# Gated linear attention and a cosine-gated feed-forward: two transposes per chunk moved from the tensor engine to the DMA queues

## The chip, the cores and the metric

The kernel runs on one core of a Trainium2 chip. The metric is the device time of one execution in microseconds (us); the time before is the median of three runs, 201.37 us (200.56 to 201.77). One execution was profiled; the engines are PE (matrix multiply; PEld are its weight loads), DVE (VectorE), ACT (ScalarE), POOL (GpSimd) and SP, which only issues DMAs and waits.

## What is computed

For each of 4 batches and 8 heads, a recurrence over 768 steps with a 48 x 48 state gives y; the heads' outputs, joined to 3072 rows of 384, pass through a feed-forward with a cosine gate. Inputs and output are float32.

```
for t in range(S):
    state = alpha[:, :, t, :, None] * state + np.einsum('bhd,bhe->bhde', k[:, :, t], v[:, :, t])
    y[:, :, t] = np.einsum('bhd,bhde->bhe', q[:, :, t], state)
...
h = x @ w_in          # 384 -> 2048
g = h * np.cos(h)
return (g @ w_out)    # 2048 -> 384
```

## The kernel before

The steps are cut into 24 chunks of 128 (six for each batch). Every chunk goes through the same units of work, and each unit is named by letters and the chunk's number j (or the pair's number g = j // 2):

- Loads on the SP queue (L98, L102): `a`, `k`, `q`, `v`, 192 KB each, 96 in all; alpha has four buffers of two chunks, the others six of one. `z` and `Z` (L109, L122) load the two weight matrices in four quarters of 768 KB each; `r`, `s`, `R` cast them to bf16.
- Decay: `i`/`l` take the logarithm of alpha on ACT (L142), `c`/`C` sum it along the chunk by a triangular matmul (L155, L159), `d`/`E` take exp of plus and minus the sum on ACT (L173, L175). `E_` (L198) keeps the last row's decay for the state.
- `K` and `Q` (L183, L189, POOL) scale k and q and write bf16 into one of three buffers, `khb` and `qhb`; `b` (L193) casts v.
- `T` (L211) transposes khb and qhb on PE, eight 128 x 128 blocks into one PSUM bank, and `t` (L217, DVE) copies the 128 x 1024 result to SBUF.
- `A` (L228) makes the scores, `m` (L237, DVE) masks them; `S` (L250) makes the chunk's contribution to the state, `u` (L262 DVE, L264 POOL) adds and decays the state; `Y` (L279, L282) makes the chunk's output from the state and the scores; `y` (L289, DVE) casts it to bf16.
- `D` (L298) transposes y on PE, three blocks, and `B` (L303, DVE) copies the result to SBUF as x.
- Feed-forward: `F` and `G` (L315) are the two halves of x @ w_in, 24 matmuls each; `f_`/`g_` (L323) the sine on ACT, `p`/`Q_` (L329) the gate on DVE; `V` and `W` (L337) the two halves of the second product, 8 matmuls each; `e` (L342, ACT) copies the result out of PSUM, and the store (L343) is issued on the SP queue.
- `w` (L353) are idle matmuls on zeros that keep PE busy at the start.

`T`, `S`, `Y` and `D` share one PSUM bank (tag `g`), the second product has one (`o`), and scores, sums and first products take turns in three buffers of two banks (`big`).

The order is written out by hand in a string, ORDER: the units are recorded in that order, and each engine, and each engine's DMA queue, takes its own ones strictly in that order. A unit starts when its engine has done the earlier ones and the semaphores it waits for have come. Eight semaphores are dealt out in turn to the DMAs that SP and ACT issue, in the order of the program, so a DMA is issued only when the one eight places before it has landed.

```
    for u in ORDER.split():
        nm = u.rstrip("0123456789")
        units[nm](int(u[len(nm):]))
```

Of the kernel before, what the change touches and what calls it, by code (L numbers as in the profile page):

```python
# [10 lines left out]
BF = mybir.dt.bfloat16  # L11
AF = mybir.ActivationFunctionType
ALU = mybir.AluOpType
# [3 lines left out]
def kernel(  # L17
# [10 lines left out]
    nc = tc.nc  # L28
    B, H, S, D = q.shape
    DM, DF = moe_w_in.shape  # L30
    C = 128
    NC = S // C
    NCH = B * NC
    NP = H // 2
    NF = DF // C
    HF = NF // 2
    HD = H * D
    CW = HD + NP
    ACOL = [(h % 2) * NP + h // 2 for h in range(H)]
    PF = 6  # L40
# [5 lines left out]
    work = ctx.enter_context(tc.tile_pool(name="work", bufs=2))  # L46
# [19 lines left out]
    qhb = consts.tile([C, 3, H, 64], BF, tag="qhb")  # L66
    khb = consts.tile([C, 3, H, 64], BF, tag="khb")
# [6 lines left out]
    ub = consts.tile([C, 3, NP, 96], BF, tag="ub")  # L74
# [3 lines left out]
    m2 = consts.tile([C, 2], FP, tag="m2")  # L78
# [5 lines left out]
    w1 = consts.tile([C, 3, DF], BF, tag="w1")  # L84
    w2f = consts.tile([C, NF, DM], FP, tag="w2f")
    w2 = consts.tile([C, NF, DM], BF, tag="w2")
# [61 lines left out]
    def cums(j0, n):  # L148
# [5 lines left out]
        for i in range(lo, lo + n):  # L154
            nc.tensor.matmul(  # L155
                cum_ps[g][:, i, 0:HD], triu_bf, lnab[:, g % 2, i, :, 0:D], start=True, stop=True
            )
            for p in range(NP):
                nc.tensor.matmul(  # L159
                    cum_ps[g][:, i, HD + p : HD + p + 1],  # L160
                    lnab[:, g % 2, i, 2 * p : 2 * p + 2].rearrange("s h d -> s (h d)"),
# [39 lines left out]
        )  # L201
        Em_t[j] = Em

    qkT_ps, qkT_t = {}, {}

    def transposes(j):
        t = ps.tile([C, 2 * NP * C], BF, tag="g")
        qkT_ps[j] = t
        for i, src in enumerate((khb, qhb)):
            for p in range(NP):  # L210
                nc.tensor.transpose(  # L211
                    t[:, (i * NP + p) * C : (i * NP + p + 1) * C],
                    src[:, j % 3, 2 * p : 2 * p + 2].rearrange("s h d -> s (h d)"), ident_bf)

    def ev_transposes(j):
        t = work.tile([C, 2 * NP * C], BF, tag="qkT", bufs=3)
        nc.vector.tensor_copy(out=t, in_=qkT_ps.pop(j))  # L217
        qkT_t[j] = t

    A_ps, A_t = {}, {}  # L220

    def scores(j):
        t = ps.tile([C, H * C], FP, tag="big", bufs=3)
        A_ps[j] = t
        for h in range(H):
            base = 64 * (h % 2)
            p = h // 2
            nc.tensor.matmul(  # L228
                t[:, ACOL[h] * C : (ACOL[h] + 1) * C],
                qkT_t[j][base : base + D, p * C : (p + 1) * C],  # L230
                qkT_t[j][base : base + D, (NP + p) * C : (NP + p + 1) * C],
                start=True, stop=True,
            )

# [7 lines left out]
        A_t[j] = t  # L242

    U_ps = {}

    def state(j):
        t = ps.tile([C, 512], FP, tag="g")
# [8 lines left out]
    def ev_state(j):  # L256

        t = U_ps.pop(j)[:, 0 : NP * 96].rearrange("r (p e) -> r p e", p=NP)
        sc = t
        if j % NC != 0:  # L260
            sc = work.tile([C, NP, 96], FP, tag="sc")
            nc.vector.tensor_tensor(out=sc, in0=t, in1=ub[:, (j - 1) % 3, :, 0:96], op=ALU.add)  # L262
        eng = nc.vector if j % NC == 0 else nc.gpsimd
        eng.tensor_tensor(  # L264
            out=ub[:, j % 3, :, 0:96].rearrange("r p (a e) -> r p a e", a=2),
            in0=sc.rearrange("r p (a e) -> r p a e", a=2),
            in1=Em_t.pop(j).unsqueeze(3).to_broadcast([C, NP, 2, D]), op=ALU.mult,
        )

    y_ps, x_t = {}, {}  # L270

    def outputs(j):
        t = ps.tile([C, 512], FP, tag="g")
        y_ps[j] = t
        first = j % NC == 0
        qT = qkT_t[j]
        for p in range(NP):
            if not first:
                nc.tensor.matmul(t[:, p * 96 : (p + 1) * 96], qT[:, (NP + p) * C : (NP + p + 1) * C],  # L279
                                 ub[:, (j - 1) % 3, p], start=True, stop=False, skip_group_check=True)  # L280
            for h in (2 * p, 2 * p + 1):
                nc.tensor.matmul(t[:, h * D : (h + 1) * D], A_t[j][:, ACOL[h] * C : (ACOL[h] + 1) * C],  # L282
                                 vpb[:, j % 3, h], start=first, stop=True, skip_group_check=True)

    y_t, xT_ps = {}, {}

    def ev_outputs(j):
        t = work.tile([C, HD], BF, tag="y_sb")
        nc.vector.tensor_copy(out=t, in_=y_ps.pop(j)[:, 0:HD])  # L289
        y_t[j] = t  # L290
        qkT_t.pop(j)
        A_t.pop(j)

    def x_transposes(j):
        t = ps.tile([C, 3, C], BF, tag="g")
        y = y_t.pop(j)
        for kt in range(3):
            nc.tensor.transpose(t[:, kt], y[:, kt * C : (kt + 1) * C], ident_bf)  # L298
        xT_ps[j] = t
# [40 lines left out]
    def ev_ff2(j):  # L340
        o_sb = moe.tile([C, DM], FP, tag="o_sb", bufs=3)
        nc.scalar.activation(out=o_sb, in_=o_ps.pop(j)[:, 0:DM], func=AF.Copy)  # L342
        nc.sync.dma_start(out=out[j * C : (j + 1) * C, :], in_=o_sb)  # L343

    w_t = []

    def warmup(n):
# [14 lines left out]
        "i": lambda j: ln(j, 1), "c": lambda j: cums(j, 1), "d": lambda j: exps(j, 1),  # L362
        "l": lambda g: ln(2 * g, 2), "C": lambda g: cums(2 * g, 2), "E": lambda g: exps(2 * g, 2),
        "K": khat, "Q": qhat, "b": vcast, "E_": emask,
        "T": transposes, "t": ev_transposes, "S": state, "u": ev_state,
        "A": scores, "m": mask_scores, "Y": outputs, "y": ev_outputs, "D": x_transposes, "B": ev_x,

# [3 lines left out]
    }  # L371

    ORDER = (
        "a0 i0 q0 q1 a1 c0 v0 d0 Q0 i1 w11 c1 d1 k0 k1 K0 w9 T0 t0 K1 a2 a3 w4 A0 v1 Q1 w1 T1 t1 b0 m0 w9 Y0 "
        "E_0 y0 A1 w2 S0 l1 C1 E1 b1 u0 q2 w1 S1 a4 a5 k2 Q2 v2 k3 E_1 E_2 l2 w9 C2 m1 E2 u1 K2 a6 a7 Y1 y1 "
        "w3 D0 b2 B0 w2 D1 B1 K3 q3 w2 S2 l3 u2 w3 T2 t2 w4 A2 Q3 T3 C3 t3 q4 Q4 m2 k4 K4 E3 w4 T4 t4 z0 s0 "
        "A3 w2 A4 z1 r1 v3 Y2 r0 s1 w1 F0 m3 m4 E_3 E_4 E_5 z2 z3 y2 F1 b3 r2 D2 B2 f_0 p0 f_1 s2 w2 S3 F2 s3 "
        "q5 u3 r3 Q5 p1 Y3 G0 G1 v4 b4 f_2 k5 y3 K5 D3 p2 B3 G2 g_0 Q_0 g_1 g_2 Z1 Z0 Y4 F3 Q_1 y4 R0 Z2 D4 "
        "G3 B4 R1 V0 f_3 T5 Q_2 F4 p3 Z3 g_3 R3 k6 K6 q6 t5 Q6 v5 v6 b5 A5 a8 S4 f_4 R2 E_6 W0 m5 a9 a10 u4 "
        "a11 b6 T6 t6 Q_3 e0 V1 W1 e1 Y5 q7 A6 l4 k7 l5 p4 y5 Q7 V2 m6 S5 K7 u5 W2 e2 q8 D5 B5 k8 k9 C4 E4 Q8 "  # L380
        "C5 S6 v7 V3 u6 Y6 y6 G4 T7 t7 K8 E5 g_4 Q_4 q9 v8 v9 F5 W3 A7 K9 q10 f_5 e3 q11 b7 b8 a12 a13 T8 p5 "
        "b9 t8 G5 m7 D6 B6 V4 g_5 E_7 Q_5 v10 a14 a15 k10 A8 S7 u7 Q9 Q10 E_8 F6 a16 k11 E_9 Y7 y7 v11 G6 m8 "
        "Q11 D7 B7 W4 S8 k12 f_6 p6 F7 u8 g_6 Q_6 E_10 T9 e4 t9 f_7 E_11 V5 l6 l7 S9 u9 p7 W5 e5 q12 q13 Y8 "
        "b10 y8 G7 K10 K11 g_7 D8 B8 A9 m9 C6 E6 T10 t10 Q_7 b11 v12 V6 a17 T11 t11 W6 e6 S10 u10 k13 k14 A10 "
        "Q12 A11 C7 m10 Y9 Q13 y9 V7 q14 m11 D9 F8 E7 l8 B9 Y10 y10 F9 v13 b12 D10 a18 W7 E_12 E_13 B10 f_8 "
        "q15 p8 v14 v15 K12 K13 S11 u11 f_9 p9 K14 q16 F10 f_10 T12 G8 g_8 t12 S12 u12 q17 k15 G9 p10 Y11 e7 "
        "k16 V8 y11 Q_8 D11 B11 a19 g_9 G10 g_10 Q_9 T13 t13 W8 C8 Q_10 K15 A12 b13 S13 Q14 e8 Q15 u13 m12 V9 "
        "T14 b14 t14 l9 W9 Y12 E8 A13 k17 E_14 k18 k19 e9 A14 a20 y12 m13 G11 Y13 y13 F11 m14 D12 B12 E_15 "
        "v16 E_16 g_11 V10 b15 Q_11 S14 u14 a21 a22 a23 f_11 K16 p11 W10 e10 T15 C9 V11 t15 D13 B13 A15 l10 "
        "F12 m15 S15 u15 E9 W11 Y14 k20 y14 f_12 p12 Q16 F13 T16 t16 G12 e11 Y15 y15 b16 v17 V12 v18 f_13 p13 "  # L390
        "E_17 D14 B14 g_12 Q_12 G13 k21 K17 D15 F14 B15 g_13 f_14 q18 q19 q20 Q17 Q_13 S16 u16 b17 W12 e12 "
        "v19 b18 A16 p14 T17 G14 G15 m16 t17 Y16 V13 y16 g_14 Q18 S17 W13 Q_14 g_15 Q_15 K18 u17 C10 E10 A17 "
        "e13 D16 B16 F15 K19 m17 S18 G16 E_18 u18 f_15 Y17 y17 K20 p15 F16 b19 q21 q22 q23 T18 t18 V14 g_16 "
        "f_16 Q19 Q20 Q21 T19 t19 W14 l11 E_19 T20 v20 Q_16 t20 C11 K21 p16 e14 V15 D17 A18 A19 E11 A20 W15 "
        "e15 B17 m18 m19 Q22 S19 u19 G17 g_17 Y18 V16 y18 D18 k22 m20 W16 B18 Y19 v21 y19 Q_17 e16 F17 T21 "
        "t21 K22 v22 v23 f_17 p17 F18 E_20 b20 S20 k23 Q23 u20 G18 f_18 g_18 D19 B19 p18 V17 E_21 E_22 A21 "
        "Y20 y20 Q_18 W17 D20 B20 m21 F19 G19 b21 Y21 e17 F20 f_19 f_20 g_19 y21 D21 V18 K23 p19 B21 p20 W18 "
        "e18 T22 t22 G20 g_20 S21 V19 Q_19 u21 T23 W19 e19 Q_20 A22 t23 A23 m22 b22 S22 u22 F21 f_21 G21 Y22 "
        "y22 m23 V20 g_21 D22 B22 p21 W20 b23 Y23 y23 e20 G22 g_22 Q_21 Q_22 D23 B23 F22 f_22 V21 W21 e21 F23 "
        "G23 p22 V22 W22 f_23 p23 g_23 Q_23 V23 W23 e22 e23 S23 E_23 u23 "  # L400
    )
    for u in ORDER.split():
        nm = u.rstrip("0123456789")
# [29 lines left out]
```

## Time and profile before

| what | value |
|---|---|
| runs | 201.37 us median, 200.56 to 201.77 |
| profiled execution | 200.76 us, span of the core 198.7 us |
| granted PE clock | 1.00 throughout |
| HBM read, written | 25.17 MB, 4.72 MB |
| DMA packets | 107034, of which 100352 under 512 B |

The span is what the profile shows between the first and the last instruction; the time of the same execution is 2.06 us longer. In the profile a line such as "L315 PE MATMUL ... x1152 | 71.2, 219 | 0.9" says: 1152 instructions of line 315, 71.2 us in which at least one of them ran, 219 ns for one by itself; matmuls overlap, so the time that one adds to a row of them is much shorter than 219 ns. After the second bar stands how long the engine had been idle before them and what ended that. "SPq" is SP's issuing of a DMA. "DMA share" is the mean busy share of the 16 DMA engines; it can read above 1.

### The profile page before, as it was taken

The page shows a single profiled execution, that of the slowest core. Times are in us where ns is not written, and L with a number is a line of the kernel's source. Part 1 is how long each engine was busy: PE and PEld are TensorE (multiplying, and loading weights), DVE is VectorE, ACT ScalarE, POOL GpSimd, SP SyncE. Part 2 cuts the span into 40 slices and gives each one's busy share as a digit, 9 for nine tenths or more (in the row PEclk, how much of TensorE's full clock was granted, in tenths as well). Part 3 has the DMA queues.
Part 4 walks back from the last instruction along what each step waited for, and adds up shares of the span by engine and source line. Part 5 has one row for each costly group of instructions (what it writes and reads, how often), then busy time and mean ns, then how long its engine had stood idle before and what let it go on. Part 6 is the DMA issues. An engine that isn't in the chain of part 4 may idle for free.

```text
span 198.7 us, 5949 instructions
## 1 busy us (share of the span) xinstructions
PE 189.0 (95%) x2544; PEld 146.1 (74%) x2549; DVE 139.9 (70%) x186; ACT 117.5 (59%) x133; POOL 78.5 (39%) x124
## 2 busy tenths in 40 slices
PE   1999998999999999999999999999999999999993
PEld 0355456897568687778878779888867978787772
DVE  6137368989754988876887956878597886759541
ACT  3233546786399447986758597467955535433450
POOL 3150881420725684565264128075922440130001
PEclk9999999999999999999999999999999999999999
DMA  6999999999988999999969945930915431111012
GB/s 129 188 186 189 168 338 353 201 379 246 193 196 169 208 175 170 240 217 177 179 145 192 177 99 113 170 79 3 196 45 120 99 66 41 43 40 42 1 43 79
DMA packets 107034, 30.27 MB, mean 152 GB/s; under 512 B 100352, under 2 KB 105472, under 8 KB 107008
## 3 DMA queue, kind: packets, MB, share of 16 engines
q1 hardware_dynamic: 107008, 29.89, 72.6%
q8 instruction: 20, 0.33, 0.8%
q14 instruction: 6, 0.05, 0.1%
HBM read 25.17 MB, written 4.72 MB: 150 GB/s over the span
## 4 chain that ended last, share of the span: by engine, by line
PE 66%; DMA 13%; SPq 11%; DVE 4%; POOL 3%; issue 2%; POOLq 0%; ACT 0%; DVEq 0%
PE o_new L337 26%; PE t L315 25%; DMA t<-in_k_dram 7%; SPq L102 7%; PE t L211 4%; DMA w1f<-in_moe_w_in_dram 4%; SPq L98 4%; PE t L228 2%; PE t L250 2%; PE t L282 2%; DMA t<-in_q_dram 2%; PE t L298 2%; DVE g_new L329 1%; PE t L279 1%; POOL khb L183 1%
## 5 line engine op out<-in xcount | busy, mean ns | idle before, releaser
L315 PE MATMUL t<-x,w 128*128 128x128 bf16 x1152 | 71.2, 219 | 0.9 <-DVE w L115 0.9
L323 ACT ACTIVATE c_sb<-t,halfpi 128x1024 bf16<-128x1024 f32 x48 | 53.0, 1112 | 31.3 <-PE t L315 31.0
L337 PE MATMUL o_new<-w,g_new 128*128 128x384 bf16 x384 | 69.4, 326 | 0.1
L315 PEld LDWEIGHTS <-w 128*128 128x128 bf16 x1152 | 65.5, 98 | 1.6 <-DVE w L115 1.2
L329 DVE TENSOR_TENSOR g_new<-t,c_sb 128x1024 bf16<-128x1024 f32 x48 | 58.0, 1216 | 6.2 <-ACT c_sb L323 6.0
L337 PEld LDWEIGHTS <-g_new 128*128 128x128 bf16 x384 | 35.3, 98 | 20.0 <-issue 0.5
L264 POOL TENSOR_TENSOR ub<-sc,Em 128x384 bf16<-128x384 f32 x20 | 16.9, 844 | 70.4 <-DVE sc L262 70.4
L183 POOL TENSOR_TENSOR khb<-t,icp_new 128x384 bf16<-128x384 f32 x24 | 23.9, 1000 | 25.1 <-DMA t<-in_k_dram 24.5
L237 DVE TENSOR_TENSOR t<-t,mask_f 128x1024 bf16<-128x1024 f32 x24 | 29.0, 1216 | 0.6 <-PE t L228 0.6
L189 POOL TENSOR_TENSOR qhb<-t,cp_new 128x384 bf16<-128x384 f32 x22 | 21.8, 1002 | 16.1 <-ACT cp_new L175 9.2
L217 DVE COPY t<-t 128x1024 bf16<-128x1024 bf16 x24 | 16.5, 688 | 13.4 <-PE t L211 13.1
L289 DVE CAST t<-t 128x384 bf16<-128x384 f32 x24 | 13.3, 556 | 17.0 <-PE t L282 16.9
L342 ACT ACTIVATE o_sb<-o_new 128x384 f32<-128x384 f32 x24 | 11.7, 489 | 22.8 <-PE o_new L337 22.4
L173 ACT ACTIVATE icp_new<-cum_new 128x768 f32<-128x768 f32 (+1 forms) x13 | 9.9, 759 | 15.5 <-PE cum_new L159 15.5
L353 PE MATMUL w_new<-warm 128*128 128x512 bf16 x64 | 18.6, 422 | 0.3 <-issue 0.2
L262 DVE TENSOR_TENSOR sc<-t,ub 128x384 f32<-128x384 f32 x20 | 11.0, 552 | 7.3 <-PE t L250 6.7
L193 POOL CAST vpb<-t 128x384 bf16<-128x384 f32 x24 | 12.5, 522 | 6.2 <-DMA t<-in_v_dram 6.1
L142 ACT ACTIVATE lnab<-a_new 128x768 bf16<-128x768 f32 (+1 forms) x13 | 10.1, 792 | 4.9 <-DMA a_new<-in_alpha_dram 4.9
L303 DVE COPY x<-t 128x384 bf16<-128x384 bf16 x24 | 8.4, 351 | 6.5 <-PE t L298 6.5
L155 PE MATMUL cum_new<-lnab,triu_bf 128*128 128x384 bf16 x24 | 7.3, 334 | 4.3 <-ACT lnab L142 4.3
L282 PE MATMUL t<-vpb,t 128*128 128x48 bf16 x192 | 11.3, 183 | 0.0
L353 PEld LDWEIGHTS <-warm 128*128 128x128 bf16 x69 | 6.4, 104 | 6.2 <-issue 2.5
(46 smaller groups left out, 167.0 us busy)
## 6 DMA issues: line engine op xcount, KB each, us to landing
a_new<-in_alpha_dram SPq DMA_DIRECT2D x24, 192.0 KB, 4.5
t<-in_q_dram SPq DMA_DIRECT2D x24, 192.0 KB, 4.3
t<-in_v_dram SPq DMA_DIRECT2D x24, 192.0 KB, 4.4
t<-in_k_dram SPq DMA_DIRECT2D x24, 192.0 KB, 4.1
out_dram<-o_sb SPq DMA_DIRECT2D x24, 192.0 KB, 2.1
w1f<-in_moe_w_in_dram SPq DMA_DIRECT2D x4, 768.0 KB, 8.3
w2f<-in_moe_w_out_dram SPq DMA_DIRECT2D x4, 768.0 KB, 8.7
```

Source lines behind the costliest of these rows:

```text
L102: nc.sync.dma_start(out=t, in_=rows(src, j))
L183: nc.gpsimd.tensor_tensor(out=khb[:, j % 3, :, 0:D], in0=k_t.pop(j), in1=icp.rearrange("s (h d) -> s h d", h=H), op=ALU.mult)
L189: eng.tensor_tensor(out=qhb[:, j % 3, :, 0:D], in0=q_t.pop(j), in1=cp[:, 0:HD].rearrange("s (h d) -> s h d", h=H), op=ALU.mult)
L217: nc.vector.tensor_copy(out=t, in_=qkT_ps.pop(j))
L237: nc.vector.tensor_tensor(out=t.rearrange("s (h t) -> s h t", h=H), in0=A_ps.pop(j).rearrange("s (h t) -> s h t", h=H), in1=mask_f.unsquee ...
L264: eng.tensor_tensor(out=ub[:, j % 3, :, 0:96].rearrange("r p (a e) -> r p a e", a=2), in0=sc.rearrange("r p (a e) -> r p a e", a=2), in1=E ...
L282: nc.tensor.matmul(t[:, h * D : (h + 1) * D], A_t[j][:, ACOL[h] * C : (ACOL[h] + 1) * C], vpb[:, j % 3, h], start=first, stop=True, skip_g ...
L315: nc.tensor.matmul(t[:, f], w1[:, kk, ft * C : (ft + 1) * C], x_t[j][:, kk], start=(kk == 0), stop=(kk == 2))
L323: nc.scalar.activation(out=c_sb, in_=h_ps[j, half], func=AF.Sin, bias=halfpi, scale=1.0)
L329: nc.vector.tensor_tensor(out=g_new, in0=h_ps.pop((j, half)), in1=c_t.pop((j, half)), op=ALU.mult)
L337: nc.tensor.matmul(o_ps[j][:, 0:DM], g[:, f], w2[:, half * HF + f], start=(f == 0 and half == 0), stop=(f == HF - 1 and half == 1))
L353: nc.tensor.matmul(w_ps, warm[:, 0:C], warm, start=True, stop=True)
```

## The change

From chunk 8 on, `T` and `t` are replaced by `Tk` and `Tq`: two DMA transposes issued on the SP queue, each of which reads khb or qhb (128 x 512 bf16) and writes 128 x 4 x 128 to a buffer of its own (three of each kind). From chunk 6 on, `D` is a DMA transpose of y (128 x 384) on the SP queue, straight into the x buffer, and `B` falls away. The stores of the result are issued by ACT instead of SP. The state is kept in slots counted without each batch's last chunk, and `S`, `u` and `E_` are no longer done for that last chunk (5, 11, 17, 23), whose state nobody reads. ORDER is written anew from its first unit to its last; the idle matmuls `w` go from 69 to 53.

```diff
+    XD = 6
...
-    qkT_ps, qkT_t = {}, {}
+    qkT_ps = {}
...
+    kT_t, qT_t = {}, {}
+
+    def dma_transpose(nm, d, src, j):
+        t = work.tile([C, NP, C], BF, tag=nm, bufs=3)
+        nc.sync.dma_start_transpose(out=t, in_=src[:, j % 3].rearrange("s h d -> s (h d)"))
+        d[j] = t
...
-                qkT_t[j][base : base + D, p * C : (p + 1) * C],
-                qkT_t[j][base : base + D, (NP + p) * C : (NP + p + 1) * C],
+                kT_t[j][base : base + D, p],
+                qT_t[j][base : base + D, p],
...
+    def us(j):
+        return (j // NC * (NC - 1) + j % NC) % 3
...
-            nc.vector.tensor_tensor(out=sc, in0=t, in1=ub[:, (j - 1) % 3, :, 0:96], op=ALU.add)
+            nc.vector.tensor_tensor(out=sc, in0=t, in1=ub[:, us(j - 1), :, 0:96], op=ALU.add)
...
     def x_transposes(j):
+        if j >= XD:
+            x = work.tile([C, 3, C], BF, tag="xT", bufs=3)
+            nc.sync.dma_start_transpose(out=x, in_=y_t.pop(j))
+            x_t[j] = x
+            return
...
-        nc.sync.dma_start(out=out[j * C : (j + 1) * C, :], in_=o_sb)
+        nc.scalar.dma_start(out=out[j * C : (j + 1) * C, :], in_=o_sb)
...
+        "Tk": lambda j: dma_transpose("kT", kT_t, khb, j), "Tq": lambda j: dma_transpose("qT", qT_t, qhb, j),
...
     ORDER = (
-        "a0 i0 q0 q1 a1 c0 v0 d0 Q0 i1 w11 c1 d1 k0 k1 K0 w9 T0 t0 K1 a2 a3 w4 A0 v1 Q1 w1 T1 t1 b0 m0 w9 Y0 "
-        "E_0 y0 A1 w2 S0 l1 C1 E1 b1 u0 q2 w1 S1 a4 a5 k2 Q2 v2 k3 E_1 E_2 l2 w9 C2 m1 E2 u1 K2 a6 a7 Y1 y1 "
-        "w3 D0 b2 B0 w2 D1 B1 K3 q3 w2 S2 l3 u2 w3 T2 t2 w4 A2 Q3 T3 C3 t3 q4 Q4 m2 k4 K4 E3 w4 T4 t4 z0 s0 "
-        "A3 w2 A4 z1 r1 v3 Y2 r0 s1 w1 F0 m3 m4 E_3 E_4 E_5 z2 z3 y2 F1 b3 r2 D2 B2 f_0 p0 f_1 s2 w2 S3 F2 s3 "
-        "q5 u3 r3 Q5 p1 Y3 G0 G1 v4 b4 f_2 k5 y3 K5 D3 p2 B3 G2 g_0 Q_0 g_1 g_2 Z1 Z0 Y4 F3 Q_1 y4 R0 Z2 D4 "
...
+        "a0 i0 q0 c0 d0 Q0 k0 k1 a1 a2 a3 q1 v0 v1 v2 i1 l1 q2 K0 w4 T0 t0 w3 c1 w9 C1 a4 d1 Q1 K1 E_0 A0 k2 "
+        "w2 T1 t1 E1 w4 A1 b0 b1 k3 a5 l2 Q2 q3 m0 S0 u0 m1 z0 w4 Y0 y0 z1 K2 z2 K3 E_1 w5 S1 u1 w3 T2 v3 t2 "
+        "w4 Y1 y1 A2 Q3 w2 T3 t3 C2 s0 b2 b3 E2 E_2 E_3 w1 A3 z3 D0 B0 m2 w2 D1 B1 r1 s1 w5 Y2 r0 w3 F0 m3 "
+        "f_0 Z1 F1 Z0 r2 Z3 y2 D2 B2 w2 S2 p0 s2 f_1 r3 F2 s3 G0 p1 G1 f_2 u2 g_0 Y3 p2 Z2 G2 k4 g_1 q4 E_4 "
...
+        "v7 G4 E_8 g_4 k7 K7 q9 k8 K8 T7 p5 q10 a12 t7 e3 G5 D6 g_5 V4 Tq8 k9 Q_4 Q_5 Tk8 S6 u6 a13 A7 W4 e4 "
+        "Q9 Q10 b7 m7 G6 g_6 K9 Y7 v8 k10 F6 v9 Tq9 y7 S7 A8 u7 Q_6 f_6 b8 V5 W5 D7 m8 Y8 l6 G7 b9 p6 y8 Tk9 "
...
+        "f_17 V16 W16 Tk19 E11 y18 K20 K21 b19 A19 p17 Tq20 e16 G17 m19 g_17 Y19 y19 D18 q21 q22 Q21 v20 Q22 "
+        "G18 g_18 S19 F18 f_18 u19 b20 Tk20 Tk21 V17 Q_17 W17 S20 Q_18 A20 p18 e17 Tq21 A21 u20 D19 k22 k23 "
...
+        "F23 f_22 W21 e21 G23 f_23 p22 V22 g_23 p23 W22 e22 Q_23 V23 W23 e23 "
     )
```

## The prediction

> **What bounds the kernel now.** I read the stages first, then the chain of waits in the first 32 us, then PE's chain, then the DMA rows.
>
> Busy time by stage (PE, PEld, DVE, ACT, POOL, then granted clock, DMA share, GB/s):
>
> ```profile
> 0.00:32.00 32.00, 25.96 (x234) 13.61 (x239) 15.91 (x30) 12.93 (x19) 14.01 (x30) 1.00 1.13 211
> 32.00:62.00 30.00, 29.47 (x421) 23.98 (x423) 24.75 (x32) 21.68 (x25) 10.39 (x14) 1.00 0.97 244
> 62.00:100.00 38.00, 37.92 (x568) 31.43 (x566) 29.60 (x39) 26.86 (x29) 20.71 (x31) 1.00 1.08 197
> 100.00:160.00 60.00, 60.00 (x872) 49.26 (x870) 46.31 (x60) 41.30 (x45) 28.41 (x43) 1.00 0.59 120
> 160.00:195.40 35.40, 35.35 (x456) 27.68 (x455) 22.77 (x27) 14.22 (x18) 4.12 (x7) 1.00 0.11 37
> ```
>
> PE never rests from 32 us to 195.4 us. DMA is full until 100 us and nearly idle after 160 us, because the loads have run ahead. The start is set by DMA; the chain of its last loads:
>
> ```profile
> 17.18 1.14 SPq L98
> ...
> 18.36 1.00 SPq L102
> ...
> 22.30 0.77 SPq L109
> ...
> 23.11 7.49 DMA w1f<-in_moe_w_in_dram
> ...
> 31.24 0.69 DVE w L115
> ```
>
> The timeline of PE where that chain ends:
>
> ```profile
> 31.98 2.85 PE L315 MATMUL t<-x,w 128*128 128x128 bf16 x48 [0.92 <-DVE w L115]
> ```
>
> The reader sees one load each 1.04 us, 21 of them before the first weight quarter, and F0 starting at 31.98 us, when the second quarter is cast. PE's chain while it is full:
>
> ```profile
> 74.40 1.34 PE t L315 x24
> 75.74 0.45 PE t L211 x8
> 76.19 1.30 PE o_new L337 x8
> 77.49 0.17 PE t L250 x4
> ...
> 80.67 0.17 PE t L298 x3
> 80.84 0.33 PE t L228 x8
> ```
>
> These are the true prices on PE: eight transposes 0.45 us, three 0.17, a state 0.17. Last, the stores and the loads, issue to landing, and a load's issue between 100 and 160 us:
>
> ```profile
> out_dram<-o_sb SPq DMA_DIRECT2D x24, 192.0 KB, 2.1
> t<-in_q_dram SPq DMA_DIRECT2D x24, 192.0 KB, 4.3
> L343 SPq DMA_DIRECT2D out_dram<-o_sb x24: 332/356/1127, 52.9 to 195.9; - x24
> ```
>
> **The change, part by part.** The sum is made against the profiled span, 198.70 us; its time is 2.06 us more, 200.76, and that is 0.61 below the median 201.37.
>
> PE. Removed: 16 x 0.45 = 7.2 us of T, 18 x 0.17 = 3.1 of D, 4 x 0.17 of S, one of which (S23) lay behind the last product: 0.5 on the path. Before, F0 to the end of W23 is 195.3 - 32.0 = 163.3 us. Ahead of F0, the new order no longer has C3 (0.6), T4 (0.45), A4 (0.33) and S2 (0.17): 1.5 us that come after it. So F0 to W23 takes 163.3 - 7.2 - 3.1 - 0.5 + 1.5 = 154.0 us if nothing waits. The idle matmuls go from 69 to 53, all but two ahead of F0, where PE waits for weights: nothing.
>
> Start. 17 loads stand ahead of the weights instead of 21: 4 x 1.04 = 4.1 us, F0 at 27.9. The other weights come earlier too: ahead of the w2 quarters three more loads (q5, v4, k5) fall away, 7 x 1.04 = 7.3 us. They landed at 41.2, 44.2, 46.3 and 48.5 (issue plus landing), now 33.9 to 41.2. New stalls: G0 stands 4.8 us of PE work behind F0, 32.7; the last w1 quarter lands at 35.9 - 4.1 = 31.8 and its casts take 1.4 (0.69 DVE, 0.63 ACT): 33.2 or a little later. V0 stands at 37.3, its second quarter lands at 36.9 and its cast takes 0.95. I put 1.0 us on each, 2.0 together.
>
> DVE loses 16 x 0.69 + 18 x 0.35 = 17 us of 139.9. It is hidden: DVE is 70% busy, and PE waited for it a few us in all, most of that for the weights' casts. POOL and DVE lose four u and E_: off the path too; the tail (3.3 us) stays, since the last store (issued at 195.9, landed 1.85 later) ends it alone.
>
> ACT. 24 store issues, each 0.36 us when the queue is idle, 1.1 when it is full: 9 to 27 us, and the new order switches the sine and logarithm tables twice more, 2 x 1.28. ACT goes from 117.5 to 129-147 us. The engine sits idle 31.3 us ahead of the sines; a sine and its gate need 0.18 + 1.11 + 1.22 = 2.5 us, and the new order leaves at least 3.4 us of PE work between F and V and 2.8 between G and W. A full-queue issue in front of the sine uses this up in chunks 19 and 20 (2.8 and 3.0): bounds 0 and 1.2 us, I take 0, as the stores' median issue is the idle one. Queued behind a store are the next sine and the next sums' exp; PE waits for them.
>
> SP queue. Before, 24 stores made it wait 73 us for ACT; these go. 50 transposes come in, each waiting in order for POOL (Tk, Tq) or DVE (D), with later loads queued behind: k9 behind Tq8, so POOL's K9. Six buffers of input cover this as long as DMA keeps ahead.
>
> DMA occupancy x of one 128 x 512 transpose: no row shows one. Below: 128 KB at the best GB/s slice (379) is 0.35 us. Above: a load is 1024 packets in 1.04 us; if a transpose's pieces were 64 B it would be 2048, 2.1 us. At 256 B pieces it is half a load, 0.52. I take 0.75, between half a load and a whole one, since these rows of short packets are nearest. The x transpose is three quarters of that, so all cost 32x + 18 x 0.75x = 45.5x. The queue in the new order: last weight lands 41.2; then 78 loads x 1.04 = 81, 24 stores x 0.5 (192 KB at 379) = 12: 134.5 + 45.5x for the last transpose, D23; behind it PE has 9.2 us and the tail 3.3. DMA's span: 147 + 45.5x, plus about 5 of holes where SP waits: 186 at 0.75. It stays 5 us under PE's.
>
> The Trainium skill speaks against the change here: "VectorE: DVE Perf Modes", section "The three transpose paths", has 390 ns for 128 x 128 on TensorE and 1309 ns by DMA, and its rules take TensorE where PSUM will do. Four such blocks, all occupying the queue, would be an estimated x = 5.2 and a span of 389 us. "DMA: Bandwidth & Descriptors", section "Latency and other measured facts", gives a transposing DMA 261 GB/s, an estimated 0.50 us per transpose: DMA at 175 us, and PE's sum stands. No run here shows either yet.
>
> Latency. x must go Y, cast, SP, DMA, F. The path needs 0.18 (matmul to DVE) + 0.56 (cast) + 0.61 (half a mask or gate ahead on DVE) + 0.5 (half an issue ahead on SP) + the landing. Landing: 2.9 us for the k load that found the queue empty, 4.3 median; I take 3.75. Need: 5.6 us. PE work between Y and the first of F, G in the new order, chunks 6 to 23: 6.2 4.8 7.3 4.8 6.4 8.0 7.5 7.2 12.0 6.5 9.4 7.1 4.7 6.3 4.5 8.0 5.7 5.3. Short: 0.8, 0.8, 0.9, 1.1 and 0.3, together 3.9 us; with a landing of 2.9, 0.2, and of 5.3, 16.4. For k and q the order has at least 9 us between S three chunks earlier (which frees khb) and A, against 1.0 (K) + 0.5 + 4.3: covered.
>
> Sum: 27.9 + 154.0 + 2.0 + 3.9 + 3.3 = 191.1 us of span, 193.2 of time.
>
> **The rivals.**
>
> 1. The DMA queue becomes the bound: slower. A transpose at 1.3 us (one and a quarter loads) gives 147 + 59 + 5 = 211 span, 213 us. It decides from x = (198.7 - 152) / 45.5 = 1.03 us, one load's price. For it: DMA share 1.08 until 100 us already, and a transpose moves short pieces, as the loads do. Against: a transpose has two thirds of a load's bytes, and after 160 us DMA has nothing to do.
> 2. Latency: transposes land 5.3 us after their issue, the worst load between 62 and 100 us, with the queue's throughput sufficient: 27.9 + 154.0 + 2.0 + 16.4 + 3.3 = 203.6 span, 205.7. With 4.5: short by 8.5, 197.8. For it: loads under a full queue take 4.4. Against: the stores, at 2.1.
> 3. ACT becomes late through its store issues and the semaphores dealt out in turn, which can make ACT wait for a transpose that SP has not issued: 1.2 us by the covers above, 194.4; no sign change.
> 4. The transposes are free and the weights on time: no stalls, 27.9 + 154.0 + 3.3 = 185.2 span, 187.3.
>
> **How the numbers follow.** A measurement of this kernel can tell about 1% from no change. Forecast (x under 0.86, where DMA's 191 meets PE's; 187 to 196): 0.47. Between that and 1.03, or latency near 4.5 (196 to 200): 0.12, two thirds of it faster by over 1%. DMA-bound (over 200): 0.34, nearly all slower. Latency at 5.3: 0.07, slower. Faster 0.47 + 0.08 = 0.55; within 1% 0.04 + 0.03 = 0.07; slower 0.38. The predicted time is 193.2; its own range is 187 to 198. The range over all reaches from 187 (rival 4) to 214 (x = 1.3), leaving out some 2 in 10, most of it above.
>
> **What would show it.** In the profile after: F0 at about 28 us; PE work without L211 after chunk 7 and without L298 after chunk 5; L315 and L337 rows as before. Right, if PE's idle time after F0 is about 6 us and DMA share is under 1 past 120 us. Wrong by rival 1, if the DMA share is 1 to the end, POOL's khb waits for k, and the score matmuls wait for transposes; by rival 2, if the share is low and L315 waits for the DMA of x; by rival 3, if gates wait for sines that stand behind L361. A median landing of transposes over 5 us would break the forecast.

## The result and the profile after

The kernel after takes 207.26 us (median of three runs, 207.22 to 209.32) against 201.37 before: ratio 1.0333, 95% interval 1.0225 to 1.0442. It is slower by 5.9 us, where 8.2 us less had been forecast. The profiled execution took 209.32 us, its span is 207.4. Here and below, a median is of all runs of a kernel; a ratio leaves disturbed runs out.

Busy time by stage of the kernel after, with the columns of the prediction's first fence (PE, PEld, DVE, ACT, POOL, granted clock, DMA share, GB/s); the first bound is F0's start and the last the end of W23:

```profile
0.00:27.70 27.70, 21.28 (x189) 11.16 (x192) 14.98 (x28) 11.09 (x16) 10.68 (x22) 1.00 1.16 219
27.70:62.00 34.30, 33.40 (x475) 26.98 (x476) 24.89 (x32) 25.39 (x28) 13.71 (x21) 1.00 1.10 250
62.00:100.00 38.00, 32.82 (x441) 26.55 (x442) 23.71 (x27) 25.53 (x28) 16.52 (x24) 0.96 0.94 168
100.00:160.00 60.00, 51.95 (x704) 39.81 (x702) 34.44 (x38) 38.56 (x43) 24.36 (x35) 1.00 1.02 173
160.00:203.90 43.90, 41.19 (x529) 32.92 (x526) 25.81 (x27) 18.59 (x21) 10.43 (x15) 0.96 0.60 106
```

Before, PE was full from 32 us to the end and DMA was nearly idle after 160 us. Now PE has holes: 0.9 us up to 62 us, then 5.2, 8.0 and 2.7, together 16.8. DMA stays near 1 until 160 us: the loads no longer run ahead. The start is as forecast: F0 begins at 27.70.

What PE itself waited for (us in all, times, the longest):

```profile
PE cum_new L156 <- ACT lnab L143: 6.0, 3, 4.6
PE t L333 <- DMA x<-t: 4.7, 5, 1.6
PE t L237 <- DMA t<-khb: 3.8, 5, 2.2
PE t L237 <- DMA t<-qhb: 2.5, 4, 0.9
```

The first line is mostly the known wait at the start (4.3 before). The three DMA lines are transposes that come late, 11.0 us, all of it after 62 us. Below them follow 4.9 us of waits for POOL, for k, q and v scaled or cast late, 2.9 of it after 62 us. Why POOL is late stands in its own waits, first after, then before:

```profile
POOL vpb L194 <- DMA t<-in_v_dram: 27.6, 9, 7.1
POOL khb L184 <- DMA t<-in_k_dram: 24.7, 11, 5.3
...
POOL qhb L190 <- DMA t<-in_q_dram: 13.8, 8, 4.0
```

```profile
POOL khb L183 <- DMA t<-in_k_dram: 24.5, 6, 8.6
...
POOL qhb L189 <- DMA t<-in_q_dram: 6.5, 2, 5.0
...
POOL vpb L193 <- DMA t<-in_v_dram: 6.1, 5, 2.4
```

The sum for k is the same, but it lies elsewhere: between 62 and 160 us POOL waits 44.9 us for loads of k, q and v, and before it waited 11.6. So loads are late too. A load that lands slowly and a load that is issued late look alike here. The issues in the page, with the median from issue to landing, tell them apart:

```profile
t<-in_k_dram SPq DMA_DIRECT2D x24, 192.0 KB, 4.6
...
x<-t SPq DMA_TRANSPOSE x18, 2.8
t<-qhb SPq DMA_TRANSPOSE x16, 3.6
t<-khb SPq DMA_TRANSPOSE x16, 3.8
```

The medians of the four kinds of load are 4.2 to 4.6 us, against 4.1 to 4.5 before (k itself 4.6 against 4.1), and transposes land faster than loads. A landing that is half a microsecond longer does not make waits of 4 to 7 us; they are issued late. The timeline of the SP queue in the middle of the run (start, duration):

```profile
119.15 1.48 SPq L310 DMA_TRANSPOSE x<-t  x1
120.74 2.14 SPq L220 DMA_TRANSPOSE t<-qhb  x1
122.97 1.16 SPq L99 DMA_DIRECT2D a_new<-in_alpha_dram  x2
124.18 0.82 SPq L103 DMA_DIRECT2D t<-in_v_dram  x1
125.10 1.66 SPq L220 DMA_TRANSPOSE t<-khb  x1
126.86 1.20 SPq L220 DMA_TRANSPOSE t<-qhb  x1
128.12 1.26 SPq L220 DMA_TRANSPOSE t<-khb  x1
129.43 0.57 SPq L103 DMA_DIRECT2D t<-in_q_dram  x1
```

Each line starts about 0.1 us or less after the one above it ends: SP does nothing but issue, and one transpose takes it about as long as two loads. Summed over SP's instructions between 62 and 160 us: before, 55.3 of 98 us in issuing (58 loads, 14 stores) and 42.7 in waiting; after, 91.3 in issuing (38 transposes 54.6 us, 48 loads 36.7) and 6.7 in waiting. All 50 transposes take SP 71.7 us. The chain of work that ended last names the same queue:

```profile
DMA 30%; SPq 28%; PE 27%; POOL 6%; issue 4%; ACT 2%; DVE 1%; ACTq 0%; POOLq 0%; DVEq 0%
```

### The profile page after: what moved, and what is told of

The parts are those of the page before. It is cut to its first block, busy times and chain, and to the rows that moved or that the text cites. A ratio compares the mean times of both kernels' runs of the same rounds, so it can differ in the third digit from the quotient of the medians.

```text
span 207.4 us, 5570 instructions
## 1 busy us (share of the span) xinstructions
PE 180.8 (87%) x2331; PEld 137.4 (66%) x2335; DVE 123.8 (60%) x148; ACT 119.6 (58%) x135; POOL 75.7 (36%) x116
## 4 chain that ended last, share of the span: by engine, by line
DMA 30%; SPq 28%; PE 27%; POOL 6%; issue 4%; ACT 2%; DVE 1%; ACTq 0%; POOLq 0%; DVEq 0%
DMA t<-in_k_dram 14%; SPq L103 13%; PE o_new L355 12%; PE t L333 11%; SPq L99 6%; DMA a_new<-in_alpha_dram 4%; DMA t<-in_q_dram 4%; POOL khb L184 3%; SPq L110 3%; DMA t<-in_v_dram 3%; SPq L123 3%; DMA t<-qhb 2%; SPq L310 2%; DMA t<-khb 2%; DMA x<-t 2%
## 5 line engine op out<-in xcount | busy, mean ns | idle before, releaser
L333 PE MATMUL t<-x,w 128*128 128x128 bf16 x1152 | 73.0, 224 | 4.7 <-DMA x<-t 4.7
L333 PEld LDWEIGHTS <-w 128*128 128x128 bf16 x1152 | 68.0, 100 | 7.2 <-DMA x<-t 2.8
L355 PE MATMUL o_new<-w,g_new 128*128 128x384 bf16 x384 | 68.4, 327 | 0.7 <-DVE g_new L347 0.5
L301 DVE CAST t<-t 128x384 bf16<-128x384 f32 x24 | 13.3, 555 | 16.8 <-PE t L294 16.2
L276 POOL TENSOR_TENSOR ub<-sc,Em 128x384 bf16<-128x384 f32 x16 | 13.3, 829 | 18.5 <-DVE sc L274 18.3
L274 DVE TENSOR_TENSOR sc<-t,ub 128x384 f32<-128x384 f32 x16 | 8.9, 554 | 11.5 <-PE t L262 11.5
L371 PE MATMUL w_new<-warm 128*128 128x512 bf16 x49 | 14.7, 418 | 0.3 <-issue 0.2
L237 PE MATMUL t<-t 48*128 48x128 bf16 x192 | 9.2, 218 | 6.3 <-DMA t<-khb 3.8
L237 PEld LDWEIGHTS <-t 48*128 48x128 bf16 x192 | 5.5, 94 | 10.6 <-DMA t<-khb 5.0
```

Source lines behind the costliest of these rows:

```text
L237: nc.tensor.matmul(t[:, ACOL[h] * C : (ACOL[h] + 1) * C], kT_t[j][base : base + D, p], qT_t[j][base : base + D, p], start=True, stop=True,)
L276: eng.tensor_tensor(out=ub[:, us(j), :, 0:96].rearrange("r p (a e) -> r p a e", a=2), in0=sc.rearrange("r p (a e) -> r p a e", a=2), in1=E ...
L333: nc.tensor.matmul(t[:, f], w1[:, kk, ft * C : (ft + 1) * C], x_t[j][:, kk], start=(kk == 0), stop=(kk == 2))
L355: nc.tensor.matmul(o_ps[j][:, 0:DM], g[:, f], w2[:, half * HF + f], start=(f == 0 and half == 0), stop=(f == HF - 1 and half == 1))
L371: nc.tensor.matmul(w_ps, warm[:, 0:C], warm, start=True, stop=True)
```

## The experiments

Theory A: SP's issuing limits the kernel after; a transpose costs SP about 1.25 us, and the queue is in order. Theory B, the prediction's first rival: the DMA engines' occupancy limits it. The profile cannot choose, as SP is 93% busy between 62 and 160 us and the DMA share there is about 1. A third way is ACT, late through its store issues.

**The price by itself (e4).** A kernel of its own issues rows of loads, rows of transposes, and pairs of one load and one transpose in three variants.

> The disputed cost by itself; nothing of the reference is computed and the output is zeros. Six stages, one after the other: 16 loads of k (192 KB) on SP; 16 transposes of 128 x 512; 16 of 128 x 384; 12 pairs of load and transpose, all on SP; the same 12 pairs with the loads issued by ScalarE; 12 pairs with a load of 128 rows of 1536 B. Theory A1 (SP's issuing is the limit): transposes come every 1.2 us with the engines idle in between; a pair takes 1.8 us on SP, 1.2 to 1.3 with the loads on ScalarE, 1.6 with long rows. Theory A2 (the engines and the closing of a transpose are the limit): a pair takes 2.0 to 2.3 us whoever issues the load, and 1.5 with long rows.

SP's timeline there (16 loads; 16 transposes of 128 x 512; 16 of 128 x 384; then two lines out of the pairs):

```profile
4.51 14.03 SPq L58 DMA_DIRECT2D ld<-in_k_dram  x16
27.26 20.91 SPq L64 DMA_TRANSPOSE tr<-src  x16
55.32 20.65 SPq L67 DMA_TRANSPOSE tr<-src  x16
...
93.93 0.58 SPq L58 DMA_DIRECT2D ld<-in_k_dram  x1
94.55 1.26 SPq L64 DMA_TRANSPOSE tr<-src  x1
```

16 transposes take 20.91 us, 1.31 each, and with a quarter less data 20.65, 1.29 each: the issue has a price of its own, not one by size. Those of 128 x 512 land 2.46 to 2.55 us after their issue, so nothing piles up behind them, and from the first issue to the last landing (27.2 to 50.0 us) the DMA share is only 0.45. That is 0.65 us of all 16 engines for a transpose; the 16 loads, counted the same way, take 1.0. A pair on SP takes 1.93 us (A1 expected 1.8, A2 2.0 to 2.3) and with long rows 1.86 (A1 1.6, A2 1.5): lighter work for the engines hardly changes it. With the loads issued by ACT the transposes still come 1.30 us apart, as A1 has it. Both prices exist: 1.26 us of SP and 0.65 of the engines.

**Half the bytes of k and q, the same issues (e18).** The kernel leaves out two of the four blocks in each transpose of k and q, and their readers read the first two again.

```diff
...
-        nc.sync.dma_start_transpose(out=t, in_=src[:, j % 3].rearrange("s h d -> s (h d)"))
+        nc.sync.dma_start_transpose(out=t[:, 0:2], in_=src[:, j % 3, 0:4].rearrange("s h d -> s (h d)"))
...
```

> The kernel after with the transposes of k and q reading 128 x 256 instead of 128 x 512 (the other two blocks are left out, and their readers read the first two again): the same 50 issues on SP, 16 x 2 half transposes less for the DMA engines. Merging two issues into one with all bytes kept gave 200.0 us. If SP's issuing alone holds the kernel after, the time stays at 206 to 209 us. If the engines' share counts as well, about 16 x 2 x 0.35 = 11 us less of their time, it falls to 200 to 204.

207.98 us, ratio 1.0301 (1.0230 to 1.0371): nothing gained. Its busy time by stage:

```profile
62.00:100.00 38.00, 32.73 (x442) 25.43 (x440) 23.31 (x26) 24.70 (x27) 15.93 (x25) 0.96 0.90 163
100.00:160.00 60.00, 54.36 (x757) 42.31 (x754) 34.89 (x39) 41.04 (x46) 23.95 (x33) 1.00 0.83 157
```

The DMA share falls from 0.94 and 1.02 to 0.90 and 0.83, the time stays. SP is as full as before the edit: 91.2 of 98 us. PE's waits for transposes are no shorter, 9.3 us for x and 3.7 for k and q, against 4.7 and 6.3. Theory B alone falls.

**The same bytes, 16 issues fewer (e10).** khb and qhb become one buffer, and one transpose of 128 x 1024 stands where the later of Tk and Tq stood.

```diff
...
+        t = work.tile([C, 2 * NP, C], BF, tag="kqT", bufs=3)
+        nc.sync.dma_start_transpose(out=t, in_=hb[:, j % 3].rearrange("s i h d -> s (i h d)"))
+        kT_t[j], qT_t[j] = t[:, 0:NP], t[:, NP:]
...
```

> The kernel after, with k and q of a chunk scaled into one buffer and transposed by one DMA of 128 x 1024 where the later of the two stood: 16 issues fewer on SP, the same bytes and the same short pieces for the DMA engines. If the issue on SP (1.25 us each, the same for three blocks as for four) limits, SP has 16 x 1.25 = 20 us less to do and the time falls to 196 to 201 us. If the DMA engines limit, nothing is saved: 206 to 209 us. If both do, coupled by SP's waits in order, it lies between, 201 to 206. Should the issue of 128 x 1024 cost 2.5 us, then issuing does go by size after all, and the time stays at 206 to 209 with the issue showing it.

199.99 us, ratio 0.9925 (0.9888 to 0.9963): 7.3 us less than the kernel after, with every byte still moved. The shortest issue of 128 x 1024 is 1.23 us, against 1.19 for half of it in the kernel after. Its stages:

```profile
62.00:100.00 38.00, 35.01 (x503) 28.14 (x503) 27.05 (x30) 28.61 (x32) 20.51 (x29) 1.00 1.10 186
100.00:160.00 60.00, 54.10 (x740) 42.13 (x739) 35.88 (x40) 40.28 (x44) 23.59 (x33) 1.00 1.08 183
```

Now DMA share is above that of the kernel after, and the issues stretch: 28 transposes take SP 47.9 us, 1.71 each. SP's waiting between issues did not fall (9.7 us, against 6.7 in the kernel after), so it is the issues that went and not the waits in order. Nor is it the clock: at a granted clock of 0.99 the kernel after took 207.22 and 207.26 us, e10 200.32 to 201.72. Theory A holds for the kernel after. That sixteen DMAs fewer also change which DMAs share a semaphore was not separated. With SP relieved, the profile points to the engines as the limit right behind it; that was not tested by itself.

**The short packets of the loads taken away (e7), and its control (e12).** Loads from chunk 6 on read 128 rows of 1536 B instead of 1024 rows of 192 B, so these chunks compute with other values.

> The changed kernel, in which the loads from chunk 6 on read 128 rows of 1536 B that lie together instead of 1024 pieces of 192 B: the same bytes in an eighth of the packets, so these chunks compute with other elements of the same tensors. By the micro stages a load of long rows takes the engines about 0.5 us instead of 0.88, and SP's issue of it behind a transpose stays at 0.58. Theory A1 (SP's issuing): nearly the time of the changed kernel, 203 to 208, with the DMA share far lower. Theory A2 (the engines): 72 x 0.4 = 28 us of engine time go, PE becomes the bound, 193 to 199.

195.51 us, ratio 0.9741 (0.9681 to 0.9801), with a DMA share of 0.81 between 62 and 100 us and 0.75 between 100 and 160.

By itself this spoke for theory B. But SP changed as well: 50 loads take 29.4 us of issuing, 0.59 each, where 48 took 36.7 before that edit, 0.76 each, and its waiting rises from 6.7 to 14.6 us. I read this as a fixed price of an issue and, when the queue is full, a wait on top, which easier loads take from SP. So e7 does not tell A from B, and e18 and e10 do.

> The kernel before, with loads from chunk 6 on that read 128 rows of 1536 B instead of 1024 of 192 B (other data, so the output is not the reference's). PE is full from 32 us on there, so a faster load should buy nothing: 200 to 202 us. If the loads limited the kernel before too, 196 to 199, and the run of the kernel after with long rows would tell less of the transposes.

In the kernel before the same edit gives 200.35 us, 0.9937 (0.9911 to 0.9964): hardly anything, where PE is the bound.

**Parts of the change (e3, e2, e1).** Transposes put back on PE in the new order: those of x (e3), of k and q (e2), all (e1). T and t stand where the later of Tk and Tq stood; in e3 and e1, D and B stand nearer to their F and G.

> Only k and q by DMA (32 transposes), x on PE. Common ground: 195.3 less 7.2 = 188.1 us of span plus stalls. Theory A (each transpose costs the queue about 1.2 us of supply): 32 x 1.2 = 38 us instead of 60, so the queue ends about 21 us earlier than in the changed kernel and PE is nearly the bound: 194 to 199 us. Theory B (the waits of D on SP for DVE are what holds the loads): also faster than the changed kernel, since these waits are gone, 194 to 199; what tells them apart is SP's issue time, which by A is still above 85 percent between 62 and 150 us, and by B falls with the loads.

> Only x by DMA (18 transposes), k and q on PE. Common ground: 195.3 less 3.1 = 192.2 us of span plus stalls. Theory A (supply: SP issues 1.2 us for each transpose and 0.57 for a load behind one, or the engines take as long; either way about 1.2 us for each): 18 x 1.2 = 22 us more work in the queue, which fits into the last third: 195 to 198 us of time. Theory B (latency and in-order waits of D on SP for DVE hold the loads behind them and F waits for x): F and G still wait for x, 6 to 10 us of waits: 201 to 205.

> The new order with every transpose back on PE (stores still by ScalarE, unread states still left out). Common ground: F0 at 27.7 us, PE work from F0 164.3 us, tail 3.3: span 195.3 plus stalls. If the slowdown comes from the DMA transposes, by whatever mechanism: stalls of 1 to 4 us, time 198 to 202, DMA idle in the last third as in the kernel before. Rival, that the new order itself or the stores on ScalarE cost the time: 205 us or more, with PE waiting after F0 for loads or for gates behind stores.

Measured: e3 201.41 us, ratio 1.0001 (0.9968 to 1.0034); e2 213.36, 1.0566 (1.0496 to 1.0635); e1 227.24, 1.1264 (1.1205 to 1.1322). I had not expected e2 and e1 to be so slow. Two of PE's waits in e1:

```profile
PE t L212 <- DVE sc L274: 3.8, 4, 1.7
PE t L262 <- DVE t L225: 2.9, 3, 1.3
```

T, S, Y and D share one PSUM bank, and the new order leaves no room for the copies that empty it: in e1 such waits for DVE's copies add up to some 17 us. These two runs tell of that order and not of the transposes. e3 is of use: 18 issues fewer on SP bring the time back to that of before, and SP then waits 12.2 us of 98.

**Loads moved to ACT (e6, e9).** Alpha and v from chunk 8 on issued by ACT, in the kernel after (e6) and in e3 (e9).

> The changed kernel, with the loads of alpha and v from chunk 8 on issued by ScalarE instead of SP: the same 32 loads, the same bytes, the same transposes. Theory A1 (SP's issuing is the limit: 1.26 us for a transpose, 0.58 for a load behind it): SP has 32 x 0.63 = 20 us less to issue; PE's work (about 154 us from F0) is then the bound with a few us of waits: 194 to 199 us. Theory A2 (the DMA engines are the limit, whoever issues): 204 to 208. A third way: ScalarE, waiting in order for semaphores that come round from SP's transposes, makes the sines late: DVE's gates wait for ScalarE by more than the 23 us of now, and the time stays over 203.

> k and q by DMA from chunk 8, x on PE (as in the earlier run, 201.4 us), and the loads of alpha and v from chunk 8 on issued by ScalarE. Theory A1: SP is left with 32 x 1.26 and 32 x 0.6 us over some 100 us, no longer a bound; what remains are the waits around x on PE: 195 to 199. Theory A2: no change, 200 to 203.

e9 takes 236.63 us, ratio 1.1752 (1.1701 to 1.1804), and e6 232.44 (228.67 to 233.52, granted clock 0.938 to 0.955; no ratio was formed). ACT in e6, then in e9, in brackets the idle time ahead of an instruction:

```profile
90.38 0.38 ACTq L104 DMA_DIRECT2D t<-in_v_dram  x1
90.84 1.28 ACT L342 ACT_TABLE_LOAD   x1 [8.06 <-DMA t<-khb]
```

```profile
116.50 6.68 ACTq L99 DMA_DIRECT2D a_new<-in_alpha_dram  x4
123.21 1.28 ACT L137 ACT_TABLE_LOAD   x1 [7.15 <-DMA t<-khb]
```

In e6 a load of the sine table, which reads no k, stood 8.06 us until a transpose of k had landed, at 90.30 us: the load of v that ACT had to issue ahead of it had been dealt the semaphore whose last user was that transpose of SP. Every sine behind it waited. In e9 the same held up a logarithm table behind four loads of alpha. The Trainium skill ("Perfetto Trace Analysis", section "DMA Optimizations") says that balancing DMAs over the engines that can issue them may help when issuing is the bottleneck. Here it was, and balancing cost 21 to 25 us (e6's fastest run and its median against the kernel after) and 35 us (e9 against e3), as the second engine had work of its own in order behind its issues.

**The stores (e13, e14, e16).** The kernel before with stores issued by ACT and nothing else (e13); the kernel after with stores on SP again (e14); e10 with each store on SP one chunk later (e16).

```diff
-        nc.sync.dma_start(out=out[j * C : (j + 1) * C, :], in_=o_sb)
+        nc.scalar.dma_start(out=out[j * C : (j + 1) * C, :], in_=o_sb)
```

> The kernel before with nothing but its stores issued by ACT instead of SP. If that part of the change is free, as the prediction has it, 200.5 to 202.5 us. If ACT's issues and its waits for semaphores delay sines, 203 to 206, with gates waiting for ACT. If SP's 73 us of waits for stores had delayed loads, 198 to 200.

> The kernel after with its stores issued by SP again, everything else as it is. The move of the stores alone cost the kernel before 2.0%. If ACT's waits for semaphores cost the kernel after as much, the time falls to 203 to 205 us. If SP's issuing is what limits it, 24 more issues of 0.36 us or more and SP's waits in order for the copies out of PSUM make it slower: 210 to 222 us.

> One transpose for k and q of a chunk (as measured at 200.0 us), with each store issued by SP one chunk later, when its data have long been there, so that neither ACT nor SP waits for anything because of a store. SP gets 24 issues (about 0.4 us each, 10 us) back, ACT loses them. If ACT's waits still cost something there, 196 to 199 us; if SP's issuing still limits, 201 to 206.

e13 takes 206.66 us, ratio 1.0204 (1.0149 to 1.0258): this part alone cost the old order 2%. Its one profiled execution, with a span of 205.0 us, shows the third way, first on ACT and then in what PE waits for:

```profile
108.33 0.34 ACTq L343 DMA_DIRECT2D out_dram<-o_sb  x1
108.70 1.28 ACT L135 ACT_TABLE_LOAD   x1 [3.97 <-DMA t<-in_k_dram]
```

```profile
PE t L315 <- ACT cp_new L175: 3.2, 1, 3.2
```

The store had been dealt the semaphore of an earlier load of k, so ACT could issue it only when that load had landed, at 108.25 us; the table load and the exponentials stood behind the store. This one wait explains 3.2 us; the rest of the difference is open.

e14 takes 242.14, ratio 1.2027 (1.1953 to 1.2101). What its SP waited for:

```profile
SPq L361 <- ACT o_sb L360: 52.1, 19, 6.6
```

Before, SP stood 73.1 us for the same copies while PE stayed full: the loads had run ahead, and SP had 42.7 us of 98 to spare. With 50 transposes behind the stores it costs 35 us: a wait on a queue is free only while nothing behind it is late. e16 takes 201.32, 0.9979 (0.9946 to 1.0011), not told apart from e10 for sure.

**The start alone (e11, e15).** The new order up to t6, then what is left in the order of before, all transposes on PE; stores by ACT (e11) or by SP (e15).

> The new order's start up to unit t6, then what is left in the order of the kernel before, every transpose on PE, stores by ACT, the four states nobody reads left out. If the earlier start is a real gain that the late part of the kernel after gives away, F0 stands at about 28 us, PE stays full to the end and the time is 195.5 to 198 us. If the start only moves the wait (loads are then late for the old order), the time is 200 to 203.

> The start of the new order spliced to the order of the kernel before, all transposes on PE, stores issued by SP as before. If the store issues by ACT took away what the earlier start gains, 196 to 199 us. If the start gains nothing when the order behind it is the old one, 201 to 203.

e11 takes 202.70 us, 1.0060 (1.0033 to 1.0086), e15 210.13, 1.0415 (1.0360 to 1.0471). Both missed what I hoped for. In e11 F0 starts at 27.53, but PE is busy only 30.5 of the 34 us from 28 to 62, where the two orders join. Against e13, which also has its stores on ACT, e11 is 1.4% better (1.0060 to 1.0204): 2.9 us, of which 0.7 are the four states left out (0.17 each). By this estimate about half of what the start gains survives the join. e15's SP waits 84.0 us for the copies out of PSUM, and ACT waits 16.9 us for loads of alpha, against 10.8 in e11 and 4.9 before.

**Only the late chunks (e8).** The order of before, stores by ACT, k and q by DMA from chunk 16 on and x from 17, when most loads are done.

> The old order, with the stores by ScalarE, and DMA transposes only where SP has little to do: k and q from chunk 16, x from chunk 17; the states of the last chunks still computed. It takes 8 x 0.45 + 7 x 0.17 = 4.8 us off PE. SP issues 23 transposes, 29 us, after 120 us, where its queue of before was idle for half of the time. If SP's issuing and its order were the fault of the changed kernel: 195 to 199 us. If a DMA transpose is late for its reader wherever it stands (issue to landing 2.5 us and more against 1.2 on PE and DVE): 200 to 204, with score matmuls or first products waiting for DMA.

202.71 us, 1.0083 (1.0051 to 1.0116). That is 1.2% better than e13, which has the same stores and no DMA transposes: there the transposes gained. Whether by the 4.8 us that they take off PE, or because the semaphores fall differently, these two runs do not tell.

**Versions with room on SP (e17, e19).** e3 with k and q merged as in e10; stores on SP one chunk later (e17) or by ACT (e19).

> k and q by one transpose per chunk from chunk 8 on, x on PE, stores issued by SP one chunk later. SP's issues per chunk: four loads and one transpose, about 3.6 us against PE's 6.5, so SP and the DMA engines have room. With k and q by two transposes and stores by ACT the time was 201.4. If SP and the semaphores were what held that back, 195 to 199 us; if it is PE with the DVE copies of x, 200 to 203.

> k and q by one transpose per chunk from chunk 8 on, x on PE, the stores by ACT: the kernel of 201.4 us with nothing but the merging, or the one of 199.75 with the stores moved back to ACT. If SP's issuing still held the first, 197 to 199.5; if PE and the DVE copies of x set the pace, 200.5 to 202.

e17: 199.75 us, 0.9907 (0.9878 to 0.9936). e19: 198.99 us, 0.9902 (0.9863 to 0.9940), the lowest median of those that compute everything, 1% ahead of the kernel before and 4% of the kernel after. SP issues for 77.4 of 98 us in e19, and PE's waits name no transposing DMA any more. Where the stores are issued makes no difference that these two can show: what e13 lost with ACT's stores in the old order is not lost in this one.

## Why the prediction was wrong, step by step

| step | predicted | measured in the kernel after |
|---|---|---|
| F0 starts | 27.9 | 27.70 |
| PE's work, F0 to end of W23 | 154.0 | 159.4 busy (155.9 in e10, at clock 1.00) |
| late weights at the start | 2.0 | 0.9 idle up to 62 us |
| late x, k, q, v | 3.9 | 15.9 idle after 62 us |
| tail | 3.3 | 3.5 |
| span | 191.1 | 207.4 |

- **Start, weights, tail: right.** 4.3 us came off the start, and the stalls behind it were less than was allowed.
- **PE's work: nearly right.** The kernel after is 5.4 us above it, of which the clock of 0.96 in two stages is 0.04 x (32.8 + 41.2) = 3.0 us. In e10, with the same instructions on PE and the clock at 1.00, it is 155.9, 1.9 above.
- **DMA occupancy: right as an estimate.** 0.75 us for a transpose was taken, e4 shows 0.65.
- **Landing: right in size; that the wait for x came out right is luck.** 3.75 was taken; the medians are 2.8 (x), 3.6 and 3.8. With 2.8 the prediction's own list of PE work falls short by less than 0.2 us in all, yet PE waited 4.7 us for x, against 3.9 forecast. The five x that it waited for were issued 2.8 to 7.1 us after their cast had ended, with SP busy issuing other DMAs, where half an issue, 0.5 us, had been allowed. Rival 2, a landing of 5.3, is out.
- **SP queue: the step that failed.** "Six buffers of input cover this as long as DMA keeps ahead" counted what the transposes wait for, and gave their issuing no price but half an issue ahead of x. The price was 1.25 us and more, 71.7 us in all, on a queue that between 62 and 160 us had 42.7 of 98 us to spare, gave up 6.6 us of stores and got 54.6 us of transposes. With nothing to spare, SP fell behind, loads went out late, POOL got k, q and v late, and scores and products waited. That k and q are "covered" fell with it: 6.3 us. The trace of before held the nearest rows for such a price, 58 loads in 48.7 us of SP, 0.84 each; the prediction never turned them into one, though it listed the 50 transposes on the queue.
- **Rival 1: right that it would be slower, and right in most of its signs, wrong in mechanism.** The scores' waits for transposes came, and POOL's waits for loads between 62 and 160 us; the DMA share was about 1 until 160 us, though 0.60 and not 1 behind that. But e18 shows that taking occupancy away does not change the time. Its break-even, an occupancy of 1.03 us, belongs to the wrong resource.
- **Rival 3, ACT: 1.2 us at most, no change of sign.** For the old order the store move alone costs 2.0% (e13), of which the semaphores that the rival names explain 3.2 us in its one profile. How much of it is in the kernel after is open: e14, which undoes it there, brings SP's wait back, and e17 and e19 see nothing.
- **The skill's estimates.** The Trainium skill, "VectorE: DVE Perf Modes", section "The three transpose paths", has 1309 ns by DMA; e4's 1.31 us is the same figure, but for one instruction of three or of four blocks, not for each block. The 261 GB/s of "DMA: Bandwidth & Descriptors", section "Latency and other measured facts", would make an estimated 0.50 us; e4's rows run at 128 KB in 1.31 us, 100 GB/s, with a DMA share of 0.45, because issuing sets their pace.

Not tried: transposes issued from two queues at once. The Trainium skill, "DMA: Bandwidth & Descriptors", section "Latency and other measured facts", says that two of them in flight from different queues corrupt each other's outputs; no run here shows it.

## What to carry to other kernels

Price a DMA three times: on the engines, on its way to landing, and on the queue that issues it; the last has a fixed part for each instruction whatever its size, so merge DMAs before moving work onto them. Where queue and engines are both near full, one profile can't say which limits: take bytes away at the same count, and take count away at the same bytes. Whether an in-order engine may wait, for a store's data or a dealt semaphore, is a property of the order around it and has to be priced anew when the order changes.

## What the runs showed of the hardware that was not expected

- The shortest issue of a transpose between SBUF buffers takes SP 1.18 us for 128 x 256 (e18) and 128 x 384, 1.19 for 128 x 512 (the kernel after) and 1.23 for 128 x 1024 (e10); in e4 a load takes 0.37 on an idle queue and 0.57 to 0.58 right behind a transpose.
- Where the DMA share is about 1, some issues get much longer: up to 3.2 us for one transpose in the kernel after and 3.8 in e10.
- The granted clock is 1.00 throughout before, and 0.96 between 62 and 100 us after, where PE was idle 5.2 of 38 us; yet it is 1.00 between 100 and 160 us, with 8.0 us idle. What sets it off is not settled.
